# Moving hashes, turns and scalings between slots of a hand-written schedule (hash attention and a gated feed-forward, one core)

## The chip, the cores and the metric

The kernel runs on one core of one Trainium2 chip. Its five engines each work through a queue of their own, in order: TensorE (PE: matmuls and their weight loads), VectorE (DVE), ScalarE (ACT), GpSimd (POOL) and SyncE (SP), which here only issues DMAs. Semaphores order the queues among each other. The metric is the device time of one execution in microseconds, as the median of several runs.

## The reference

Inputs are q, k, v with 4 batches, 8 heads, 768 tokens and 64 values per head, a projection of 64 x 6, and the weights of a feed-forward block (512 to 1536 to 512).

```python
q_bits = (q @ proj > 0);  k_bits = (k @ proj > 0)      # 6 bits per token and head
mask   = bucket(q_bits)[..., :, None] == bucket(k_bits)[..., None, :]
scores = where(mask, q @ k.T / 8, -1e9)
attn   = softmax(scores)                               # 1e-9 added to the sum
x      = (attn @ v) as (4 * 768, 8 * 64)
xn     = x / sqrt(mean(x * x) + 1e-6) * rms_g
out    = (silu(xn @ w_gate) * (xn @ w_val)) @ w_out     # (3072, 512), float32
```

## The kernel before, in words

**Halves and slots.** Each batch b is done in two halves of 384 query tokens, w = 2b and 2b + 1, so there are eight halves. A *slot* is one of 192 steps: one head of one half, and one third p of the 768 keys (two blocks of 128). `SLOTS` lists them in order; heads go in pairs hp = 0 to 3. In the first four halves the pairs of two halves are interleaved (`TURNS`): half 2 takes slots 48 to 53 and 60 to 77, half 3 takes 54 to 59 and 78 to 95, and half 2 comes to pair 3 at slot 72. From half 4 on each half has 24 slots in a row. In step s the loop at the end of the kernel emits the scores of slot s + 1 (`scores`, two matmuls), then the planned work of rank below 3, then the exponentials of slot s + 1 (`probs`, ScalarE), then the rest of the plan by rank. Every engine's order follows from that list: `at(s, f, ...)` puts a piece of work into slot s. Nothing reorders it later.

**Masks by extra rows.** q and k stand transposed in a tile `QK` per pair: 64 rows of values and 12 rows of sign bits, scaled so that a score with a differing bit is pushed far down. The work on one pair (b, hp) before its first scores is:

- `load_blocks`: k and q as four DMAs each, issued by SyncE; v as one.
- `turn_dve`: eight transposes on VectorE, four for k and then four for q, one per slot (`in_row`), into `kT` and `qT`.
- `cast_pool`: copies to fp16 into `QK` on GpSimd; `v_prep` and `v_sum` there too.
- a hash: matmuls of `kT` and `qT` with the projection into a bank `d_ps` (line 210), their signs on VectorE (`bits`, line 217), then DMAs of the bits into the rows of `QK`, issued by SyncE. `hash_lone` (batch 1) hashes one pair with eight DMAs (line 285); `hash_pairs` (batches 2 and 3) hashes two pairs at once with eight (line 303).

`in_row(loads, s, hash_slot)` gives the slots: loads of k, q, v; turns at s to s + 7; casts at s + 4 and s + 8, v at s + 9; the hash at `hash_slot` (for batches 2 and 3 only at the odd pair, for both).

**Feed-forward.** When a half's eight heads are done, `attn_out` has divided by the softmax sum (`otmp`, `rcp` on VectorE, `x` and `sq` mostly on GpSimd); `norm` makes `rstd`; `scale_x` (VectorE, line 424) makes `xn`; `turn_x` transposes it on TensorE (`x_ps`) and VectorE writes `xnT`. From slot s0 = 24 w + 42 on, `gate` and `value` (lines 446 and 456) run over 12 blocks of columns between the scores of the following halves, from s0 + 16 on `project` (line 469), whose three results per half are copied by ScalarE to `ysb` and stored by a DMA that SyncE issues (line 478). So the first half's feed-forward starts at slot 42, its three stores are planned at slots 60, 63 and 66; the second half's starts at slot 66.

SyncE has all loads of q, k, v, all DMAs of bits and nearly all stores in one queue, in the order of the slots. GpSimd's queue issues the weight loads (lines 520 and 526).

Banks for `g_ps`, `v_ps`, `d_ps`, `x_ps`, `y_ps` and `m_ps` come from one pool of three; scores have two of their own, `o_ps` one.

Of the kernel before, what the change touches and what calls it, by code (L numbers as in the profile page):

```python
# [44 lines left out]
def kernel(  # L45
# [530 lines left out]
    def at(s, f, *a, rank=3):  # L576
        plan[s].append((rank, len(plan[s]), lambda: f(*a)))
# [55 lines left out]
    def in_row(loads, s, hash_slot=None):  # L633
        return loads, range(s, s + 8), (s + 4, s + 8, s + 9), hash_slot

    work = {
        (1, 1): in_row((21, 32, 33), 42, 50), (1, 2): in_row((38, 42, 44), 50, 58),
        (1, 3): in_row((46, 50, 53), 58, 66),
        (2, 0): in_row((56, 60, 62), 66), (2, 1): in_row((63, 67, 70), 74, 82),
        (2, 2): in_row((72, 75, 78), 82), (2, 3): in_row((80, 84, 87), 90, 98),  # L640
        (3, 0): in_row((90, 94, 98), 100), (3, 1): in_row((100, 104, 108), 110, 119),
        (3, 2): in_row((116, 120, 124), 126), (3, 3): in_row((126, 130, 134), 136, 145),
    }
# [34 lines left out]
    for w in range(8):  # L678
        for h in range(H):
            end = LAST[w, h] + 3  # L680
            at(end - 1, av, w, h, 0, 9)
            at(end, av, w, h, 9, 18)
            if h % 2:
                at(end, o_step, w, h // 2, rank=4.5)
                if (w, h) != (0, 7):
                    late = 3 if h == 7 and w < 3 else 5 if (w, h) == (0, 5) else 4
                    at(end + late, s_step, w, h // 2, rank=5 if late != 5 else 4)
        s0 = 24 * w + 42
        n0 = {0: 9, 2: 7}.get(w, 11)
        at(s0 - n0, norm, w, rank=5)  # L690
        for c in range(3):
            at(s0 - {0: 4, 2: 6 - c}.get(w, 8 - c), scale_x, w, c, rank=5)
            xs = {0: (2, 1, 1), 2: (4, 2, 1)}.get(w, (5, 3, 1))
            at(s0 - xs[c], turn_x, w, c, rank=1)
        seen = set()
        for ft in range(NF):
            for f, s in ((g_step, s0 + 16 * ft // NF), (v_step, s0 + (32 * ft + 16) // (2 * NF))):
                at(s, f, w, ft, rank=4 if s in seen else 2)
                seen.add(s)
        for i in range(9 if w < 7 else 6):  # L700
            c, j = divmod(i, 3)
            at(s0 + 16 + i, project, w, c, 4 * j, 4 * j + 4, rank=1 if i == 8 else 3)
# [61 lines left out]
```

## Time and profile before

| | |
|---|---|
| median of 3 runs | 346.21 us (344.65 to 346.27) |
| the profiled execution | 345.11 us, its span 343.3 us |
| TensorE busy | 330.0 us (96%) |
| VectorE, ScalarE, GpSimd busy | 238.6, 208.1, 156.4 us |
| granted TensorE clock, mean | 0.99 |

All times in the rows below are microseconds from the start of the span. A row of the timeline gives start, duration, engine, line, operation, what is written and read, and how many instructions are merged in it; in square brackets the idle time of the engine before it and what ended it. "SPq" is SyncE issuing DMAs: its duration is the issue, not the transfer. A row of the waits gives who waited for whom, the total, how often, and the longest. A row of the windows gives the stretch, then the busy time of PE, PEld, DVE, ACT and POOL, each with its number of instructions, then the granted clock, the DMA share and GB/s. In the chain of waits, a DMA piece runs from the start of its issue to its landing.

### The profile page before, as it was taken

Reading aid. Unit: us, or ns where it says so; the run is one execution under the profiler, and the core shown is the slowest. Engines: PE = TensorE matmul, PEld = TensorE weight load, DVE = VectorE, ACT = ScalarE, POOL = GpSimd, SP = SyncE. Lnnn points to the kernel's source line nnn. Section 1 sums busy time; section 2 is a strip of 40 time slices with the busy share of each in tenths; the row PEclk is TensorE's granted clock in tenths of the full one; section 3 lists DMA queues with packets and bytes.
Section 4 is the critical chain, followed back from the end, with each engine's and each line's share of the span. In section 5 each row is a group of like instructions: output and inputs, shape, how many; then the busy total and the mean of one; then the engine's idle time right before and its main releaser. Section 6 shows DMA issues by size and latency. Waiting matters only on the chain.

```text
span 343.3 us, 7798 instructions
## 1 busy us (share of the span) xinstructions
PE 330.0 (96%) x2983; PEld 201.4 (59%) x2983; DVE 238.6 (70%) x532; ACT 208.1 (61%) x324; POOL 156.4 (46%) x230
## 2 busy tenths in 40 slices
PE   8999979999969999999999999999999999999995
PEld 7566646555535645666565665656566656655653
DVE  4789669888564977788868695877446753784860
ACT  3789967665544745757666675667667765532322
POOL 4888775487631775636836156353101221130000
PEclk9999999999996999999999999999999999999999
DMA  7998939947375904803631373000010001001002
GB/s 239 324 235 183 139 57 186 161 78 141 72 170 112 170 7 96 193 5 85 148 83 29 63 140 107 33 6 13 32 61 2 3 31 63 0 3 61 32 0 92
DMA packets 85972, 31.36 MB, mean 91 GB/s; under 512 B 71480, under 2 KB 82992, under 8 KB 85936
## 3 DMA queue, kind: packets, MB, share of 16 engines
q1 hardware_dynamic: 82000, 26.09, 32.9%
q0 software_dynamic: 3712, 4.72, 9.1%
q8 instruction: 23, 0.38, 0.4%
q14 instruction: 13, 0.11, 0.1%
q10 hardware_dynamic: 224, 0.07, 0.1%
HBM read 28.32 MB, written 6.29 MB: 101 GB/s over the span
## 4 chain that ended last, share of the span: by engine, by line
PE 83%; DVE 8%; ACT 3%; SPq 2%; DMA 2%; issue 1%; DVEq 0%; ACTq 0%
PE v_ps L456 16%; PE y_ps L469 16%; PE s_ps L344 15%; PE g_ps L446 13%; PE o_ps L366 9%; PE d_ps L210 4%; PE s_ps L446 3%; ACT psb L354 2%; PE t_ps L170 2%; DVE t L457 1%; DVE ht L458 1%; DMA vL<-in_v_dram 1%; PE x_ps L431 1%; PE z_ps L337 1%; DVE kT L194 1%
## 5 line engine op out<-in xcount | busy, mean ns | idle before, releaser
L354 ACT ACTIVATE psb<-s_ps 128x768 f16<-128x768 f32 x192 | 150.6, 809 | 32.3 <-PE s_ps L344 30.3
L344 PE MATMUL s_ps<-QK 76*128 76x384 f16 x384 | 94.4, 328 | 4.9 <-DMA QK<-bits 3.0
L456 PE MATMUL v_ps<-xnT,wv 128*128 128x384 f16 x384 | 78.9, 328 | 0.0
L448 ACT ACTIVATE t<-g_ps 128x384 f32<-128x384 f32 x78 | 38.3, 491 | 54.0 <-PE g_ps L446 53.5
L469 PE MATMUL y_ps<-wo,ht 128*128 128x512 f16 x276 | 69.2, 379 | 0.0
L446 PE MATMUL g_ps<-xnT,wg 128*128 128x384 f16 x312 | 64.8, 330 | 1.3 <-DVE xnT L432 0.8
L366 PEld LDWEIGHTS <-psb 128*128 128x128 f16 x1152 | 52.4, 98 | 22.5 <-issue 4.7
L457 DVE SCALAR_TENSOR_TENSOR t<-t,g_ps 128x384 f32<-128x384 f32 x78 | 42.7, 548 | 32.3 <-ACT t L448 31.9
L390 POOL TENSOR_TENSOR x<-otmp,rcp 128x384 f32<-128x384 f32 x31 | 25.9, 837 | 82.1 <-DVE rcp L386 81.8
L458 DVE SCALAR_TENSOR_TENSOR ht<-t,v_ps 128x384 f16<-128x384 f32 x96 | 53.2, 554 | 11.9 <-PE v_ps L456 2.6
L366 PE MATMUL o_ps<-vl,psb 128*128 128x65 f16 x1152 | 57.0, 194 | 0.0
L446 PEld LDWEIGHTS <-wg 128*128 128x128 f16 x384 | 36.5, 98 | 26.0 <-issue 3.2
L456 PEld LDWEIGHTS <-wv 128*128 128x128 f16 x384 | 36.4, 98 | 24.7 <-issue 2.1
L344 PEld LDWEIGHTS <-QK 76*128 76x128 f16 x384 | 31.6, 98 | 21.8 <-issue 9.0
L469 PEld LDWEIGHTS <-ht 128*128 128x128 f16 x276 | 25.8, 97 | 24.8 <-issue 1.2
L202 POOL CAST QK<-qT 64x768 f16<-64x768 f32 x22 | 18.2, 829 | 26.6 <-DVE qT L194 23.8
L476 ACT COPY ysb<-y_ps 128x512 f32<-128x512 f32 x23 | 13.5, 587 | 24.4 <-PE y_ps L469 24.0
L402 POOL TENSOR_TENSOR sq<-x 128x384 f32<-128x384 f32 x31 | 25.8, 831 | 2.4
L432 DVE TENSOR_TENSOR xnT<-x_ps,gcol 128x512 f16<-128x512 f16 x24 | 16.2, 681 | 14.8 <-PE x_ps L431 14.8
L381 DVE TENSOR_TENSOR otmp<-o_ps,cvb 128x390 f32<-128x390 f32 x32 | 17.9, 559 | 9.9 <-PE o_ps L366 9.8
L202 POOL CAST QK<-kT 64x768 f16<-64x768 f32 x22 | 18.2, 826 | 10.6 <-PE v_ps L456 4.0
L194 DVE STREAM_TRANSPOSE kT<-kL 128x192 f32<-128x192 f32 x44 | 22.2, 519 | 0.0
(80 smaller groups left out, 304.6 us busy)
## 6 DMA issues: line engine op xcount, KB each, us to landing
vL<-in_v_dram SPq DMA_DIRECT2D x16, 384.0 KB
out_dram<-ysb SPq DMA_DIRECT2D x23, 256.0 KB
kL<-in_k_dram SPq DMA_DIRECT2D x44, 96.0 KB
qL<-in_q_dram SPq DMA_DIRECT2D x44, 96.0 KB
kL<-in_k_dram SPq DMA_DIRECT2D x4, 384.0 KB
qL<-in_q_dram SPq DMA_DIRECT2D x4, 384.0 KB
wg<-in_moe_w_gate_dram POOLq DMA_DIRECT2D x2, 768.0 KB, 7.4
wv<-in_moe_w_val_dram POOLq DMA_DIRECT2D x2, 768.0 KB, 8.1
```

The lines of the kernel that those rows point to most:

```text
L202: nc.gpsimd.tensor_copy(QK[b, hp][0:64, hh, o : o + S], T0[b, hp, which][64 * hh : 64 * hh + 64, :])
L344: nc.tensor.matmul(ps[:, j, 0:HALF], k_cols(w // 2, h, 2 * p + j), q_cols(w, h), start=True, stop=True,)
L354: nc.scalar.activation(psb[w, h][:, p], sps.pop(g)[:, :, 0:HALF], AF.Exp, scale=ESCALE,)
L366: nc.tensor.matmul(o[:, c, hh, 0:65], psb[w, h][:, jt // 2, jt % 2, 128 * c : 128 * c + 128], vls[b % 2][:, h, v_chunk(b, h, jt), 0:65], s ...
L390: eng.tensor_mul(xd.rearrange("p c (h d) -> p c h d", h=2), tmp[:, :, :, 0:64], r.to_broadcast([128, 3, 2, 64]),)
L402: nc.gpsimd.tensor_mul(sq, xd, xd)
L446: nc.tensor.matmul(g, wg[:, kt, fs], xnT[w][:, kt], start=(kt == 0), stop=(kt == 3))
L448: nc.scalar.activation(t, g, AF.Tanh, scale=0.5)
L456: nc.tensor.matmul(vv, wv[:, kt, fs], xnT[w][:, kt], start=(kt == 0), stop=(kt == 3))
L457: nc.vector.scalar_tensor_tensor(out=t, in0=t, scalar=1.0, in1=g, op0=ALU.add, op1=ALU.mult)
L458: nc.vector.scalar_tensor_tensor(out=ht[w][:, ft], in0=t, scalar=0.5, in1=vv, op0=ALU.mult, op1=ALU.mult)
L469: nc.tensor.matmul(y, ht[w][:, ft, c * 128 : (c + 1) * 128], wo[:, ft, :], start=(ft == 0), stop=(ft == NF - 1),)
```

## The change

Only slots in the plan change; the work itself is the same.

```diff
     work = {
-        (1, 1): in_row((21, 32, 33), 42, 50), (1, 2): in_row((38, 42, 44), 50, 58),
-        (1, 3): in_row((46, 50, 53), 58, 66),
-        (2, 0): in_row((56, 60, 62), 66), (2, 1): in_row((63, 67, 70), 74, 82),
-        (2, 2): in_row((72, 75, 78), 82), (2, 3): in_row((80, 84, 87), 90, 98),
+        (1, 1): in_row((21, 32, 33), 42, 51), (1, 2): in_row((38, 42, 44), 49, 58),
+        (1, 3): in_row((46, 52, 54), 56, 65),
+        (2, 0): in_row((56, 60, 62), 64), (2, 1): in_row((63, 66, 69), 72, 81),
+        (2, 2): in_row((71, 75, 78), 81), (2, 3): in_row((80, 83, 86), 89, 98),
         (3, 0): in_row((90, 94, 98), 100), (3, 1): in_row((100, 104, 108), 110, 119),
...
         for c in range(3):
-            at(s0 - {0: 4, 2: 6 - c}.get(w, 8 - c), scale_x, w, c, rank=5)
-            xs = {0: (2, 1, 1), 2: (4, 2, 1)}.get(w, (5, 3, 1))
+            at(s0 - {0: 5 - c // 2, 2: 6 - c}.get(w, 8 - c), scale_x, w, c, rank=5)
+            xs = {0: (3, 2, 1), 2: (4, 2, 1)}.get(w, (5, 3, 1))
             at(s0 - xs[c], turn_x, w, c, rank=1)
```

Each hash of batches 1 and 2 now stands two slots behind the last turn of its pair, where it stood one (except the double hash of (2,2) and (2,3), which moves from one to two as its turns move). For that the hash of (1,1) moves a slot later, those of (1,3) and of (2,0) with (2,1) a slot sooner, and the rows of turns of (1,2), (2,2) and (2,3) one slot, of (1,3), (2,0) and (2,1) two slots sooner; the casts and the preparation of v move with them. A few loads move by one or two slots. In SyncE's queue one thing changes places: the eight DMAs of the bits of (1,3) stand ahead of the first half's third store, which stood ahead of them.

For the first half (w = 0) two of the three scalings move from slot 38 to 37, ahead of the other half's `otmp` and `rcp` on VectorE; the third stays behind these at 38. The transposes move from slots 40, 41, 41 to 39, 40, 41.

## The prediction

> **What bounds the kernel now.** I read the page's head first, then TensorE's waits, then windows over the stretch where it waits longest, then the DMA queue of SyncE through that stretch.
>
> ```profile
> span 343.3 us, 7798 instructions
> PE 330.0 (96%) x2983; PEld 201.4 (59%) x2983; DVE 238.6 (70%) x532; ACT 208.1 (61%) x324; POOL 156.4 (46%) x230
> ...
> PE s_ps L344 <- DMA QK<-bits: 3.0, 1, 3.0
> PE s_ps L344 <- ACT psb L354: 1.4, 5, 0.4
> PE d_ps L210 <- DVE qT L194: 1.1, 2, 0.7
> ...
> PE g_ps L446 <- DVE xnT L432: 0.8, 1, 0.8
> PE x_ps L431 <- DVE xn L424: 0.6, 1, 0.6
> ...
> PE g_ps L446 <- DVE t L457: 0.4, 1, 0.4
> ...
> 99.00:102.30 3.30, 0.34 (x3) 0.11 (x2) 1.77 (x4) 0.56 (x1) 1.62 (x2) 0.94 0.40 141
> 102.30:109.30 7.00, 7.00 (x33) 3.54 (x33) 2.44 (x5) 3.07 (x5) 0.00 (x0) 0.54 0.37 61
> ...
> 150.00:200.00 50.00, 50.00 (x471) 30.46 (x469) 37.95 (x82) 32.61 (x51) 26.02 (x36) 1.00 0.38 82
> ```
>
> TensorE is busy 96% of the span, so a step counts only where it takes away an idle stretch of TensorE or a slow one. The waits (columns: total us, times, longest) are few, and four of the six quoted stand where the change moves work: `x_ps` and `g_ps` at slots 40 to 42, `d_ps` at the two hashes whose last turn is one slot ahead of them, and `s_ps` waiting 3.0 us for sign rows of a hash. The windows (TensorE's busy time is the second number, the granted clock the third from the end) show that this last wait costs twice: behind it the clock is 0.54 for 7.00 us, in which TensorE is busy throughout. At full clock that work takes 0.54 x 7.00 = 3.78 us, so the slow stretch costs 3.22 us beside the wait's 2.96. From 150 us on TensorE is simply full: time won before stays won.
>
> Why that one wait ends when it does is the question on which the forecast turns:
>
> ```profile
> 98.45 0.81 PE L456 MATMUL v_ps<-xnT,wv 128*128 128x384 f16 x4
> 102.22 0.80 PE L344 MATMUL s_ps<-QK 76*128 76x384 f16 x2 [2.96 <-DMA QK<-bits]
> ...
> 76.95 2.71 SPq L122 DMA_DIRECT2D qL<-in_q_dram  x4
> 79.76 0.59 SPq L112 DMA_DIRECT2D vL<-in_v_dram  x1
> 80.45 3.10 SPq L122 DMA_DIRECT2D kL<-in_k_dram  x4
> 83.67 6.21 SPq L285 DMA_DIRECT2D QK<-bits  x8
> 89.92 2.71 SPq L122 DMA_DIRECT2D qL<-in_q_dram  x4
> 92.72 0.58 SPq L478 DMA_DIRECT2D out_dram<-ysb  x1
> 93.35 0.42 SPq L112 DMA_DIRECT2D vL<-in_v_dram  x1
> 93.87 3.38 SPq L122 DMA_DIRECT2D kL<-in_k_dram  x4
> 97.36 1.06 SPq L478 DMA_DIRECT2D out_dram<-ysb  x2
> 98.50 6.61 SPq L285 DMA_DIRECT2D QK<-bits  x8
> ...
> 98.04 0.38 SPq L478 DMA_DIRECT2D out_dram<-ysb  x1
> ...
> 91.92 0.68 DVE bits L217
> ...
> 100.20 1.88 DMA QK<-bits
> ```
>
> The bits of pair (1,3) are there at 91.92 + 0.68 = 92.60. Their eight DMAs start to be issued at 98.50. In between SyncE is not waiting, it is issuing: each row begins where the one before ends, back to 76.95 and beyond. The scores need the third of the eight, whose issue starts at 100.20 and which has landed 1.88 us later, at 102.08. So the wait is ended by a queue 5.9 us behind its data, not by the hash.
>
> **The change, part by part.**
>
> *Scalings of the first half (scale_x(0, 0) and (0, 1) from slot 38 to 37, turn_x a slot sooner).*
>
> ```profile
> 43.95 0.89 POOL L419 TENSOR_TENSOR rstd<-ms,mhalf 128x3 f32<-128x3 f32 x1
> 45.32 0.56 DVE L381 TENSOR_TENSOR otmp<-o_ps,cvb 128x390 f32<-128x390 f32 x1 [1.83 <-PE o_ps L366]
> 46.03 2.38 DVE L424 TENSOR_SCALAR xn<-x,rstd 128x512 f16<-128x512 f32 x3
> 48.34 1.87 DVE L432 TENSOR_TENSOR xnT<-x_ps,gcol 128x512 f16<-128x512 f16 x3
> ...
> 50.26 0.81 PE L446 MATMUL g_ps<-xnT,wg 128*128 128x384 f16 x4 [0.80 <-DVE xnT L432]
> ...
> L424 DVE TENSOR_SCALAR xn<-x,rstd x24: 402/484/1057, 46.0 to 310.1; 128x512 f16<-128x512 f32 x24
> ```
>
> VectorE stands idle 1.83 us ahead of the other half's `otmp`, and rstd is ready at 44.84. Put first, two scalings run there at 0.40 to 0.48 us each (the shortest and the median of the 24), to about 45.8; `otmp` and the reciprocal follow to 46.55, 0.45 later than now, the third scaling to about 47.1, the three `xnT` (1.87) to about 49.1. The first gate starts near 49.15 instead of 50.26: 1.1 us won, between 0 (if `otmp`, 0.45 late, holds back the next half) and 1.4 (both idle times of the page's rows above, 0.6 and 0.8). It reaches the end only if nothing behind it waits for something else, and the wait at 102.22 does.
>
> *Hash of pair (1,1) at slot 51 instead of 50, that of (1,2) still at 58 with its turns a slot sooner.* The second takes the smaller of the two `d_ps` waits away, 1.1 - 0.7 = 0.4 us, ahead of 102.22 as well. The first costs nothing: its bits are there at 64.09 + 0.68 = 64.77 and SyncE issues them from 69.87, so a slot more (well under 2 us) is hidden there.
>
> ```profile
> 64.09 0.68 DVE L217 TENSOR_SCALAR bits<-d_ps,thr,scl 128x384 f16<-128x384 f32 x1 [0.96 <-PE d_ps L210]
> ...
> 69.87 6.98 SPq L285 DMA_DIRECT2D QK<-bits  x8
> ```
>
> In slots 42 to 57 VectorE gets 18 turns for 16; two more at some 0.5 us each fit into what TensorE has won there.
>
> *Hash of pair (1,3) at slot 65, turns from 56.* The bits come about 3 us sooner, which SyncE does not notice. What it notices is the order: the third store of the first half (slot 66) now stands behind the eight DMAs instead of ahead of them. They start 98.50 - 98.04 = 0.46 sooner, and so does the landing: the wait ends near 101.76. The lower bound is 0 (one of the two weight loads on the other queue, issued sooner, takes transfer time from SyncE's loads), the upper 1.06, both stores' issue. I take 0.46, by the row itself. The other loads keep their order on SyncE; (1,3)'s q and v loads go from 50 and 53 to slots 52 and 54, the q load now behind (1,1)'s hash as it was.
>
> TensorE meets the wait with 1.1 + 0.4 us more in hand. So the idle stretch begins near 97.7 instead of 99.26 and is about 4.0 us long; what was won before 98 goes into it, with no gain at the end.
>
> *The q turns of (1,3), slots 60 to 63 instead of 62 to 65,* come close to their load. Its last issue ends at 79.66; the nearest landing is the 1.88 from issue start to data, so it is there at 80.9 (the v load's 4.35 in the chain would make it 83.4). The turn of slot 60, now the third k turn of (1,3), stands at 80.41, after the change near 78.9. VectorE can wait 2.0 us there, at most 4.5, with the third scaling and an `otmp` behind it. TensorE has the 4.0 us stretch in front of it: cost 0, as long as less than that is passed on.
>
> ```profile
> 135.36 4.35 DMA vL<-in_v_dram
> ...
> 80.41 0.52 DVE L194 STREAM_TRANSPOSE kT<-kL 128x192 f32<-128x192 f32 x1
> ...
> 121.72 0.53 DVE L457 SCALAR_TENSOR_TENSOR t<-t,g_ps 128x384 f32<-128x384 f32 x1
> ...
> 123.39 0.51 PE L210 MATMUL d_ps<-qT,pq 128*32 128x384 f32 x1 [0.69 <-DVE qT L194]
> ...
> SPq L303 <- DVE kT L194: 8.2, 1, 8.2
> ```
>
> *Batch 2: turns of (2,0) to (2,3) one or two slots sooner, the double hash at slot 81 instead of 82.* Here the wait of 0.69 at 123.39 goes: the last q turn is two slots ahead. Late next is the second bank, free when `t` has been formed (121.72 + 0.53 = 122.25), while TensorE would have finished the first bank at about the same time. So I take 0.6, bounds 0 and 0.69. It is behind the SyncE wait, and TensorE is full from there on, so it stays. SyncE itself idles 8.2 us at that hash now: its DMAs a slot sooner cost nothing. The hash of (2,2) and (2,3) stays at 98 and had no wait. On GpSimd the preparation of v of (2,3) goes ahead of one normalisation; that engine has idle time on both sides, cost 0.
>
> *The clock.* The slow stretch was worth 3.22 us. I leave it as it is, with 1.6 either way (half of it): the idle time ahead of it grows, its end does not move by more than 0.46.
>
> The Trainium skill (TensorE: Matmul & The Clock Gate, Part 1) says that the gate halves the clock after an idle window of about 3.4 us, counted freely, and lifts it after a busy one. The trace agrees on the halving (0.50 to 0.54), though here 2.96 us of idle time were already enough. By that rule a stretch longer than a window is throttled in every run, where a shorter one may slip between two windows.
>
> **Sum.** 345.11 (span 343.30 and 1.81 around it) - 0.46 - 0.6 = 344.05, with 1.1 + 0.4 won and lost again in the SyncE wait. The median of the runs shown is 346.21, 0.3% above the profiled one; 0.997 of it is 345.1. I forecast 345.1. Its own range: lower 343.0 (1.06 + 0.69 and the clock 1.4 better), upper 347.0 (nothing won, clock 0.8 worse).
>
> **Rivals.**
> - *The wait goes altogether.* If the hash, not the queue, were late, 2.96 + 3.22 + 0.6 would go: 338.3, or 339.4 by the median. For it: the hash is done 3 us sooner. Against it: the eight DMAs would have to start some 4 us sooner, and SyncE's rows leave 0.46. A tenth.
> - *The longer idle stretch holds the clock down longer (slower).* Place: from 97.7. The low clock lasted some 7 us; if it lasts another such stretch, TensorE loses 0.46 x 7.00 = 3.2 more: 347.3, by the median 348.4. It decides once the extra slow time is over 2 x 1.06 us. For it: 4.0 us is a third more than what brought the throttle on. Against it: the added idle time is itself spent before the matmuls resume, so part of the slow time falls into it. 0.13.
> - *VectorE's wait for (1,3)'s q load is passed on.* It decides beyond 4.0 us of delay; at the 4.5 bound, with the two extra turns, 1.5 us are left: about 346.6 by the median's scale if the gains stay, 347.7 if the 0.6 and 0.46 go too. Against: TensorE there runs projections and scores, which do not read VectorE's turns. 0.09.
> - *The main case,* a small gain from an order of two DMAs and one hash: 0.68.
>
> **The numbers.** Half a per cent, 1.73 us, is about what a measurement can tell. Faster by more (below 344.5): the first rival 0.10 and three tenths of the main case, 0.20. Slower by more (above 347.9): the clock 0.10, VectorE 0.04, main 0.02. The rest, 0.54, is within. For the range I leave out the first rival's 0.10 and some 0.09 at the top: 341.5 to 348.0.
>
> **What would show it.** Right: SyncE's eight DMAs for (1,3) start near 98.0 with one store ahead of them; `s_ps` waits about 4 us for them; the first gate starts near 49.2; no `d_ps` wait on qT. Wrong: an `s_ps` wait shorter than 2.9 us, which would mean that SyncE's queue follows the work it serves; a low clock of over 8 us; a `g_ps` or `o_ps` wait on VectorE between 80 and 97 that outlasts the DMAs.

## The result and the profile after

| | before | after |
|---|---|---|
| median of 20 runs each | 344.31 us (340.43 to 346.27) | 340.82 us (339.42 to 343.79) |
| profiled execution | 345.11 us, span 343.3 | 340.95 us, span 339.2 |
| granted clock, mean | 0.990 | 0.995 |

After takes 0.9917 of before, 95% interval 0.9892 to 0.9943: 0.8% faster. The forecast was 345.1 (341.5 to 348.0), so the time lies below the range.

The head of after's page, and TensorE's waits:

```profile
span 339.2 us, 7797 instructions
PE 326.1 (96%) x2983; PEld 200.2 (59%) x2983; DVE 237.7 (70%) x532; ACT 207.9 (61%) x324; POOL 155.6 (46%) x230
...
PE d_ps L210 <- DVE t L457: 3.5, 1, 3.5
PE s_ps L344 <- DMA QK<-bits: 1.3, 2, 1.1
...
PE g_ps L446 <- DVE xnT L432: 0.6, 1, 0.6
```

Windows of after (columns as in the prediction) over its new wait on `d_ps`, the stretch ahead of slot 72, the 7 us behind it, and all from the scores of slot 72 to the end:

```profile
66.70:71.00 4.30, 4.27 (x27) 1.98 (x28) 3.84 (x9) 0.81 (x1) 2.74 (x4) 0.60 0.95 190
99.00:102.30 3.30, 1.81 (x18) 1.06 (x18) 2.97 (x8) 1.19 (x2) 1.38 (x2) 1.00 0.30 96
102.30:109.30 7.00, 6.77 (x63) 4.34 (x63) 4.52 (x11) 4.28 (x7) 4.33 (x6) 1.00 0.33 75
102.23:339.20 236.97, 232.91 (x2032) 140.76 (x2032) 162.03 (x338) 139.28 (x222) 87.23 (x116) 1.00 0.28 62
```

The last of these windows in before:

```profile
102.22:343.30 241.08, 236.71 (x2032) 142.29 (x2032) 161.89 (x338) 139.53 (x222) 87.39 (x116) 0.99 0.26 59
```

The scores of slot 72 begin at 102.22 before and 102.23 after. Everything won ahead of them is gone by then. All of the profiled gain lies behind: 241.08 - 236.97 = 4.11 us, with the same 2032 matmuls.

The timelines of after, of TensorE, SyncE and VectorE:

```profile
48.54 0.81 PE L446 MATMUL g_ps<-xnT,wg 128*128 128x384 f16 x4 [0.57 <-DVE xnT L432]
66.73 0.56 PE L210 MATMUL d_ps<-kT,pk 128*32 128x384 f32 x1 [3.48 <-DVE t L457]
102.23 0.49 PE L344 MATMUL s_ps<-QK 76*128 76x384 f16 x2 [1.07 <-DMA QK<-bits]
118.76 0.51 PE L210 MATMUL d_ps<-kT,pk 128*32 128x384 f32 x1
120.53 1.03 PE L469 MATMUL y_ps<-wo,ht 128*128 128x512 f16 x4
...
50.45 8.08 SPq L122 DMA_DIRECT2D kL<-in_k_dram  x4
79.33 4.38 SPq L122 DMA_DIRECT2D kL<-in_k_dram  x4
94.09 3.69 SPq L122 DMA_DIRECT2D kL<-in_k_dram  x4
97.88 0.58 SPq L478 DMA_DIRECT2D out_dram<-ysb  x1
...
65.77 0.52 DVE L194 STREAM_TRANSPOSE kT<-kL 128x192 f32<-128x192 f32 x1 [4.33 <-issue]
```

The chain of after at the new wait:

```profile
55.60 5.84 DMA kL<-in_k_dram
61.44 4.33 issue
65.77 0.52 DVE kT L194
```

The same turn in the timeline of before:

```profile
66.57 0.89 DVE L194 STREAM_TRANSPOSE kT<-kL 128x192 f32<-128x192 f32 x2
```

GpSimd's issue of the second of the two loads of `w_out` (768 KB each), in the timelines of before and of after:

```profile
59.41 0.89 POOL L526 DMA_DIRECT2D wo<-in_moe_w_out_dram  x1
```

```profile
57.72 0.89 POOL L526 DMA_DIRECT2D wo<-in_moe_w_out_dram  x1
```

Here is the wait that the prediction didn't have. The first k turn of (1,2) stands one slot sooner (49), and TensorE reaches that slot 1.7 us sooner. The turn needs all four k loads of its pair, which are issued from 50.45 to 58.53. The chain goes back to the last of them, though it names nothing for the last 4.33 us. The semaphore records in the trace do: the fourth load's last step comes at 65.69, and VectorE's queue is held ahead of this turn until 65.72. So VectorE stands idle for those 4.33 us, a `t` and the hash of (1,1) are queued behind the turn, and TensorE waits 3.48 us at 66.73 and then runs at a clock of 0.60. Before, the turn started at 66.57, later than it does now, and without idle time.

The slot alone doesn't make this wait. By the same records the fourth load had landed at 61.64 in before; a turn ready at 61.44, as it is in after, would have waited 0.2 us for that. In after it lands 4.05 us later. What stands otherwise around it is the weight load of the two rows above: it too comes 1.69 us sooner, and so before the fourth k load's issue has ended (58.53; in before the issue had ended at 58.38, ahead of the weight load). In the nine profiled kernels with the scalings moved, the weight load is issued at 57.59 to 58.10, and the k load lands at 65.67 to 66.76 in eight of them, at 61.61 in the ninth (e10 below). In the six without, it is issued from 58.79 on, and the k load has landed by 61.74 in all. That the weight load holds the k load up is argued from this order; no run moves it alone.

The stall costs nothing at the end, since the scores of slot 72 start at 102.2 anyway. It only takes up the time that was won, and more: at slot 72 there are 1.07 us left to wait instead of 2.96, and the clock behind is 1.00.

The starts of the 96 gates in order, after less before, show the same as a running account: -1.7 us at gates 1 to 7, +3.2 at 9 to 12 (the new wait), -0.26 at the gate at 102.81, -2.76 from the gate at 109.86 to the 24th, -4.00 at the 25th, -4.15 from the 32nd to the end. So 2.76 us come from the clock behind slot 72 (the scores there start at the same time), 1.23 from the stretch with the hash at slot 81, and about 0.14 from one near the hash at slot 98. The loss of the clock at 66.7 isn't in the sum, as it falls ahead of the wait.

### The profile page after: what moved, and what is told of

It reads as the page before. It is cut to its first block, busy times and chain, and to the rows that moved or that the text cites. A ratio compares the mean times of both kernels' runs of the same rounds, so it can differ in the third digit from the quotient of the medians.

```text
span 339.2 us, 7797 instructions
## 1 busy us (share of the span) xinstructions
PE 326.1 (96%) x2983; PEld 200.2 (59%) x2983; DVE 237.7 (70%) x532; ACT 207.9 (61%) x324; POOL 155.6 (46%) x230
## 3 DMA queue, kind: packets, MB, share of 16 engines
HBM read 28.32 MB, written 6.29 MB: 102 GB/s over the span
## 4 chain that ended last, share of the span: by engine, by line
PE 80%; DVE 8%; POOL 3%; DMA 3%; SPq 2%; issue 2%; ACT 1%; DVEq 0%; ACTq 0%; POOLq 0%
PE y_ps L469 18%; PE v_ps L456 16%; PE s_ps L344 14%; PE g_ps L446 13%; PE o_ps L366 8%; PE d_ps L210 4%; PE s_ps L446 3%; DMA kL<-in_k_dram 2%; PE x_ps L431 1%; SPq L122 1%; SPq L285 1%; PE z_ps L337 1%; PE t_ps L170 1%; DMA QK<-bits 1%; DVE t L457 1%
## 5 line engine op out<-in xcount | busy, mean ns | idle before, releaser
L446 PE MATMUL g_ps<-xnT,wg 128*128 128x384 f16 x312 | 63.5, 325 | 1.2 <-DVE xnT L432 0.6
```

The costliest lines, as they stand in the source:

```text
L446: nc.tensor.matmul(g, wg[:, kt, fs], xnT[w][:, kt], start=(kt == 0), stop=(kt == 3))
```

## The experiments

Three theories. *Queue:* the scores of slot 72 are released by SyncE's queue; what is won ahead of them is lost, and gains come only from the clock behind and from later steps. *Parts:* each part keeps its own gain to the end. *Stall:* the new wait at 66.73 costs time, and without it the change would be worth far more.

### Which part brings it

**e1_scalings: before, with the scalings' part alone.**

```diff
-            at(s0 - {0: 4, 2: 6 - c}.get(w, 8 - c), scale_x, w, c, rank=5)
-            xs = {0: (2, 1, 1), 2: (4, 2, 1)}.get(w, (5, 3, 1))
+            at(s0 - {0: 5 - c // 2, 2: 6 - c}.get(w, 8 - c), scale_x, w, c, rank=5)
+            xs = {0: (3, 2, 1), 2: (4, 2, 1)}.get(w, (5, 3, 1))
```

> The kernel before with the scalings of the first half alone moved. Queue theory (the scores of slot 72 start at about 102.2 us whatever is won ahead of them, since SyncE's queue brings their sign rows; what counts is whether a long idle stretch ends there and leaves a low clock behind it): the first gate starts near 48.6 instead of 50.26, the scores of slot 72 still between 101.5 and 102.8, with an idle stretch of 2.5 us or more and the low clock behind it; time against before 0.995 to 1.005. Stall theory (each wait taken away gains its own length): 1.7 us faster, 0.995, with the scores of slot 72 near 100.5.

343.47 us, 0.9978 [0.9950, 1.0006]. The first gate starts at 48.62, 1.64 us sooner. The timeline of this kernel at slot 72, and the window behind:

```profile
101.84 0.80 PE L344 MATMUL s_ps<-QK 76*128 76x384 f16 x2 [3.48 <-DMA QK<-bits]
```

```profile
101.84:108.84 7.00, 7.00 (x41) 3.88 (x42) 2.44 (x6) 3.13 (x5) 0.00 (x0) 0.59 0.33 55
```

The wait is longer than the 2.96 of before, the scores start only 0.38 sooner, and the clock behind is low as before. Of the 1.64 us won, 0.52 went into this wait, as the queue theory has it. Another 0.74 was lost ahead of it, most of it at the turns of (1,2): they still stand at slot 50 here, but their k load lands late (65.91), and VectorE waits 1.03 us for it.

**e2_batch1: before, with the rows of (1,1), (1,2), (1,3) alone.**

```diff
-        (1, 1): in_row((21, 32, 33), 42, 50), (1, 2): in_row((38, 42, 44), 50, 58),
-        (1, 3): in_row((46, 50, 53), 58, 66),
+        (1, 1): in_row((21, 32, 33), 42, 51), (1, 2): in_row((38, 42, 44), 49, 58),
+        (1, 3): in_row((46, 52, 54), 56, 65),
```

> The kernel before with the rows of turns and hashes of batch 1 alone moved. Queue theory: VectorE's first turn of pair (1,2), a slot sooner, waits for its k load, TensorE waits for VectorE near 65 us, and the idle stretch at the scores of slot 72 is under 2 us with no low clock behind it; these scores start at 101.5 to 102.8; some 3 us faster, 0.989 to 0.994. Stall theory: the d_ps wait of 0.4 us goes, 0.999.

343.45 us, 0.9976 [0.9947, 1.0006]: less than expected. Without the scalings the k load of (1,2) is there in time (61.56): its first turn, at slot 49 as in after, starts at 62.60 without a wait. So the move of the turns alone doesn't stall VectorE, and the wait at slot 72 stays at 2.56 us. In the profiled execution the clock didn't drop behind it, as the timelines of VectorE and TensorE and the window show:

```profile
62.60 0.54 DVE L194 STREAM_TRANSPOSE kT<-kL 128x192 f32<-128x192 f32 x1
...
101.65 0.48 PE L344 MATMUL s_ps<-QK 76*128 76x384 f16 x2 [2.56 <-DMA QK<-bits]
```

```profile
101.65:108.65 7.00, 7.00 (x65) 4.50 (x66) 4.25 (x9) 4.28 (x7) 1.59 (x2) 1.00 0.39 85
```

That execution has a span of 339.7, but most runs of this kernel have a lower mean clock, so the median gains little.

**e3_batch2: before, with the rows of batch 2 alone.**

```diff
-        (2, 0): in_row((56, 60, 62), 66), (2, 1): in_row((63, 67, 70), 74, 82),
-        (2, 2): in_row((72, 75, 78), 82), (2, 3): in_row((80, 84, 87), 90, 98),
+        (2, 0): in_row((56, 60, 62), 64), (2, 1): in_row((63, 66, 69), 72, 81),
+        (2, 2): in_row((71, 75, 78), 81), (2, 3): in_row((80, 83, 86), 89, 98),
```

> The kernel before with the rows of batch 2 alone moved (double hash at slot 81). Both theories: the d_ps wait of 0.69 us near 123 goes, nothing else moves; 0.998, with the idle stretch and the low clock at the scores of slot 72 as in the kernel before. If batch 2 carries the gain, 0.992.

342.70 us, 0.9951 [0.9921, 0.9982], more than expected. Between the 24th and the 25th gate it gains 1.23 us, as the whole change does. The scores of slot 72 even start later than before here (103.12, after 3.80 us). The three parts add up to -0.22 - 0.24 - 0.49 = -0.95%, the whole is -0.83%. Each interval is about 0.3% either way, so the parts add up within the noise; batch 2's is the only one of the three that is clear of 1. These times alone don't tell the theory of parts from that of the queue; e1's rows do.

**e8_hash82: before, with the turns of (2,1) one slot sooner and the hash left at slot 82**.

```diff
-        (2, 1): in_row((63, 67, 70), 74, 82),
+        (2, 1): in_row((63, 67, 70), 73, 82),
```

> The kernel before with one row alone changed: pair (2,1) turns from slot 73 instead of 74, its hash still at 82, so two slots behind the last turn. The wait of 0.69 us near 123 goes, and with it 0.5 us in which the four matmuls of that hash did not run side by side: 1.2 us between the twelfth gate of the second half and the first gate of the third (17.77 in the kernel before, 16.5 here). The scores of slot 72 as before. If the place of the hash between value and projection matters, not the wait, then 17.8.

344.63 us in its one run, span 342.9. From the 24th to the 25th gate it gains 0.72, not the 1.2 expected: the `d_ps` wait is gone, but an `x_ps` wait of 0.57 has come at 129.96. The first of the bank's sixteen matmuls (four run side by side) and the projection behind them, in the timeline of this kernel and then of before:

```profile
122.11 0.51 PE L210 MATMUL d_ps<-kT,pk 128*32 128x384 f32 x1
...
123.60 1.04 PE L469 MATMUL y_ps<-wo,ht 128*128 128x512 f16 x4
```

```profile
121.85 0.51 PE L210 MATMUL d_ps<-kT,pk 128*32 128x384 f32 x1
...
124.80 1.04 PE L469 MATMUL y_ps<-wo,ht 128*128 128x512 f16 x4
```

The stretch takes 123.60 - 122.11 = 1.49 us here and 124.80 - 121.85 = 2.95 before, where only 0.69 was shown as a wait. In after it takes 120.53 - 118.76 = 1.77. In before six of the sixteen ran ahead of the wait and ten behind it. So the wait and the split together cost nearer 1.2 to 1.5 us than 0.69; how the rest comes about, the rows don't say.

### Is it the clock?

**e4_filler and e4b_filler: before, with 40 idle matmuls (the kernel's own filler, line 337) ahead of the scores of slot 72.** Their results are used by nothing.

```diff
-{0: 8, 3: 6}.get(g, 0)
+{0: 8, 3: 6, 72: 40}.get(g, 0)
```

> The kernel before with 40 idle matmuls of 128 columns put ahead of the scores of slot 72 (the helper that the kernel has for its start), nothing else moved. Queue theory: the scores of slot 72 start at about 102.2 as before, TensorE is busy until shortly before, the clock stays at 1.0 behind it, and the 3.2 us of slow work go: 0.989 to 0.993, as much as the whole change. Stall theory: no wait is shorter, so 1.000, or slower by what the fillers take.

> The kernel before with the 40 idle matmuls ahead of the scores of slot 72, once more for a profile. The scores still start between 101.6 and 103.1; the idle time of TensorE ahead of them is under 1 us; no low clock behind them; the gates after them follow at the pace of the full clock. Time 0.994 to 0.999 against before, as the first look at this edit had it.

343.32 us, 0.9968 [0.9937, 0.9998], and 343.61 us, 0.9966 [0.9926, 1.0006]. The trace of the first has a clock of 0.66 from end to end, so no row of it is read. The second, its timeline and the window behind:

```profile
98.31 2.40 PE L337 MATMUL s_ps<-ones 128*128 128x128 f16 x40
103.41 0.80 PE L344 MATMUL s_ps<-QK 76*128 76x384 f16 x2 [2.70 <-DMA QK<-bits]
104.00 1.49 PE L446 MATMUL g_ps<-xnT,wg 128*128 128x384 f16 x4
```

```profile
104.00:108.00 4.00, 4.00 (x21) 2.17 (x20) 0.61 (x2) 1.95 (x3) 0.00 (x0) 0.50 0.26 43
```

The expectation of less than 1 us of idle time was missed: the fillers ran early, the DMAs came later in this execution, and 2.70 us were left, with the low clock behind them. Over all the runs it is clearer. The mean clock of a run comes in steps of about 0.005, which is 0.005 x 340 = 1.7 us. In the traces that is one stretch of 3.41 us at half the clock; before has two of them behind slot 72 (101.93 to 108.76), after one behind its new wait. Counted in such steps:

| mean clock | before: runs, median | after: runs, median |
|---|---|---|
| 0.998 and over | 12, 341.78 us | 2, 339.74 us |
| about 0.995 | 46, 344.04 us | 11, 340.95 us |
| about 0.990 | 32, 345.56 us | 7, 340.91 us |

These are the 92 runs of before that stand beside the experiments; two more of them have 0.985, at 347.3 and 348.4 us. In before a step costs 1.5 to 2.3 us. In after there are as many steps (1.25 per run), but in the medians the second costs nothing; that fits the profile, where one falls ahead of the wait at slot 72. The fillers cut the steps from 1.26 per run to 0.36 and 0.7 and brought 0.3%, at the edge of the noise and less than the steps' price: at full clock they themselves cost something (their runs without a step have medians of 342.75 and 342.43 us, against 341.78). That the clock makes up part of the gain is shown by the table and the profiles together; the fillers alone don't show how much.

### Does the new stall cost anything?

**e5_turn50: after, with the turns of (1,2) back at slot 50, the hash at 59.**

```diff
-        (1, 2): in_row((38, 42, 44), 49, 58),
+        (1, 2): in_row((38, 42, 44), 50, 59),
```

> The changed kernel with one row put back: pair (1,2) turns from slot 50 again (hash at 59), so that VectorE no longer waits for its k load and TensorE no longer for VectorE near 63 us (3.48 us in the changed kernel). Queue theory: what is won there is lost at the scores of slot 72, which start at 101.5 to 103.1 as in all kernels so far, with 3 us or more of idle time ahead and a low clock behind, where it counts: 1 to 2 us slower than the changed kernel, 0.993 to 0.998 against before. Stall theory: 3.5 us and its low clock gained, 0.978 to 0.983.

341.59 us, 0.9910 [0.9880, 0.9940]: as fast as after. But the edit didn't take the stall away. The load of (1,2), landed at 66.76, still holds VectorE up, for 2.80 us, and the bits of (1,1) behind it hold TensorE for 2.25. So the 0.978 to 0.983 of the stall theory weren't put to the test. What the run shows is that TensorE's wait near 67 is 1.23 us shorter than in after, and that at slot 72 is 1.89 us longer:

```profile
66.84 0.52 DVE L194 STREAM_TRANSPOSE kT<-kL 128x192 f32<-128x192 f32 x1 [2.80 <-DMA kL<-in_k_dram]
67.87 0.81 PE L446 MATMUL g_ps<-xnT,wg 128*128 128x384 f16 x4 [2.25 <-DVE bits L217]
102.69 0.49 PE L344 MATMUL s_ps<-QK 76*128 76x384 f16 x2 [2.96 <-DMA QK<-bits]
```

### Can the queue be relieved?

**e6_act and e7_act_turn50: after, and after with e5's edit, with the k and q loads of (2,0) issued by ScalarE.**

```diff
+            if which != "v" and (b, hp) == (2, 0):
+                at(s, load_blocks, nc.scalar, b, hp, which)
+                continue
```

> The changed kernel with the eight k and q loads of pair (2,0) issued by ScalarE (same slots, 56 and 60) instead of SyncE. Queue theory: SyncE reaches the sign rows of (1,3) 5 to 6 us sooner, near 93; the scores of slot 72 then start when TensorE gets there, 101.2 instead of 102.23, and later stages keep the 1 us: 0.986 to 0.990 against before. Should the queue not be what holds them, nothing moves: 0.992.

> Both edits: (2,0)'s k and q loads on ScalarE's queue and (1,2)'s turns at slot 50, hash at 59. Queue theory: with the queue no longer behind, the 3.48 us at 63 and the low clock after them now count, so the edit that loses alone wins here: scores of slot 72 start at 97 to 99, no slow window there; 0.974 to 0.984 against before. If the two edits only added (1 us gained and 1.5 lost), 0.990 to 0.995.

344.22 us, 1.0015 [0.9988, 1.0042], and 344.95 us, 1.0035 [1.0011, 1.0060]: 1% slower than after. SyncE was relieved, but the issue now stands in ScalarE's queue, whose activations TensorE needs. Of e7, ScalarE's queue and activations, then TensorE:

```profile
75.47 4.25 ACTq L122 DMA_DIRECT2D kL<-in_k_dram  x4
79.83 0.49 ACT L448 ACTIVATE t<-g_ps 128x384 f32<-128x384 f32 x1 [6.29 <-DMA kL<-in_k_dram]
...
81.23 0.80 PE L344 MATMUL s_ps<-QK 76*128 76x384 f16 x2 [5.00 <-issue]
```

For the queue theory these two settle nothing, as they put a new bound in place of the old one.

**e9_noload: e5 with the q load of (2,0) left out.** The q turns of (2,0) read its k tile instead, so that part of the scores is another one.

```diff
-        src = raw[b, hp, which]
+        src = raw[b, hp, "k" if (b, hp) == (2, 0) else which]
...
+            if (b, hp, which) == (2, 0, "q"):
+                continue
```

> The kernel with (1,2)'s turns at slot 50 (its scores of slot 72 at 102.69 behind 2.96 us of idle time), and the four q DMAs of pair (2,0) left out: that pair's q is turned from its k tile, so its scores are not the reference's, with the same work on every engine but SyncE. Queue theory: the eight sign DMAs of (1,3) start 2.7 us sooner, near 96.3, the scores of slot 72 at 99.7 to 100.3, idle under 0.8 us, no low clock behind: 0.980 to 0.986 against before. If something else held these scores, they stay at 102 to 103 and the time at 0.991.

336.47 us, 0.9770 [0.9732, 0.9808], better than expected. The DMAs of (1,3)'s bits start at 94.10, TensorE waits for bits 0.19 us at most, and no run has a low clock. Four loads fewer on SyncE bring 1.4% against e5, where the whole change brought 0.8%. In the profile VectorE's wait for (1,2)'s k load is still there (landed at 65.67), with 1.35 us of it left on TensorE.

**e10_late: e5 with the first half's first two stores and the v load of (2,0) moved behind those DMAs, to slot 66.** Nothing is left out. TensorE waits for none of the three; once the v load is moved, GpSimd waits 3.58 us for it, up to 105.19.

```diff
+    def late_stores():
+        for dst, src in held_out:
+            nc.sync.dma_start(out=dst, in_=src)
...
-            nc.sync.dma_start(out=rows[:, out_chunk(w, c), :], in_=ysb)
+            if w == 0 and c < 2:
+                held_out.append((rows[:, out_chunk(w, c), :], ysb))
+            else:
+                nc.sync.dma_start(out=rows[:, out_chunk(w, c), :], in_=ysb)
...
-        (2, 0): in_row((56, 60, 62), 64),
+        (2, 0): in_row((56, 60, 66), 64),
...
+    at(66, late_stores)
```

> The kernel with (1,2)'s turns at slot 50, and three DMAs that nobody waits for moved behind the sign DMAs of (1,3) on SyncE's queue: the first half's first two stores and the v load of (2,0). Nothing is left out. Queue theory: those sign DMAs start 1.8 us sooner, near 97.2, the scores of slot 72 at 100.6 to 101.3, idle 1 to 1.6 us, a low clock behind it rarely: 0.983 to 0.989, better than both kernels. If the wait were for anything but the queue, 0.991.

**336.44 us, 0.9780 [0.9738, 0.9822]**: faster than both kernels. Its span, TensorE's wait for bits, and SyncE's queue:

```profile
span 334.8 us, 7797 instructions
...
PE s_ps L344 <- DMA QK<-bits: 0.2, 1, 0.2
```

```profile
88.75 2.71 SPq L122 DMA_DIRECT2D qL<-in_q_dram  x4
91.50 2.72 SPq L122 DMA_DIRECT2D kL<-in_k_dram  x4
94.33 6.17 SPq L285 DMA_DIRECT2D QK<-bits  x8
100.60 0.61 SPq L485 DMA_DIRECT2D out_dram<-ysb  x1
...
104.83 1.23 SPq L466 DMA_DIRECT2D out_dram<-ysb  x2
```

The two stores of L466 are the ones moved; L485 is the first half's third. In this execution (1,2)'s k load landed at 61.61, and VectorE didn't wait for it.

**e11_wide: e10, with (1,2)'s bits in four DMAs of 768 columns instead of eight** (its hash over two banks).

```diff
-                at(sh, hash_lone, b, hp)
+                at(sh, hash_wide if hp == 2 else hash_lone, b, hp)
```

> The same, and the hash of (1,2) over two banks so that its sign rows need four DMAs of 768 columns instead of eight of 384: 2.9 us less on SyncE's queue, 0.8 us more on TensorE and 0.6 us more on VectorE at slot 59. Queue theory: sign DMAs of (1,3) start near 94.3, the scores of slot 72 when TensorE gets there, 100.3 to 100.9, no idle time over 0.5 us: 0.982 to 0.988, no better than moving the three DMAs alone by more than 0.003, since what the queue gives back TensorE has paid at the hash.

336.69 us, 0.9774 [0.9734, 0.9814]. The DMAs of (1,3) start at 92.88, 1.45 sooner again, and it brings nothing. TensorE no longer waits there, so a shorter queue has nothing left to give; that the hash over two banks costs TensorE what the queue gives back, as expected, would look the same.

**e12_before_late and e13_after_late: e10's edit of the three DMAs on before and on after.**

> The kernel before with the first two stores and the v load of (2,0) moved behind the sign DMAs of (1,3), without any of the change's moves. Queue theory: those DMAs start 1.7 us sooner or more, the scores of slot 72 at 99.3 to 100.7 with under 1.4 us of idle time and hardly a low clock behind: 0.984 to 0.991 against before. The waits at 48 to 50, 76 and 123 us stay, so it is slower than the kernel that has both by 2 to 4 us. If the change's moves carried the 0.978 of that kernel, and not the queue, this one stays within 0.995 to 1.000.

> The changed kernel, (1,2)'s turns at slot 49 and its hash at 58 as it has them, with the same three DMAs moved behind. Queue theory: the 3.5 us that TensorE waits near 63 and the low clock after them are no longer taken up by a later wait, so they count: scores of slot 72 at 100.5 to 101.5, 2 to 4 us slower than with the turns at slot 50, 0.984 to 0.990 against before; the same difference of one slot was worth nothing (0.991 and 0.992) while the queue was behind. Stall theory: the one-slot difference is worth the same here as there, nothing: 0.978.

339.73 us, 0.9877 [0.9828, 0.9925], and 337.77 us, 0.9832 [0.9779, 0.9886]. The timelines of e12, then timeline and window of e13. The e13 execution shown is the slowest of its six (340.45 us); four of the six have a mean clock of 0.998 or more, at 336.74 to 337.83 us, so what it shows of the clock isn't the usual case:

```profile
96.84 6.19 SPq L285 DMA_DIRECT2D QK<-bits  x8
100.50 0.48 PE L344 MATMUL s_ps<-QK 76*128 76x384 f16 x2 [1.02 <-DMA QK<-bits]
```

```profile
66.79 0.85 PE L210 MATMUL d_ps<-kT,pk 128*32 128x384 f32 x1 [3.65 <-DVE t L457]
```

```profile
66.79:71.00 4.21, 4.21 (x25) 1.79 (x26) 3.62 (x9) 0.81 (x1) 2.68 (x4) 0.50 1.00 200
```

| ratio to before | old order of SyncE | three DMAs moved |
|---|---|---|
| before's slots | 1 | 0.9877 |
| the change | 0.9917 | 0.9832 |
| the change, turns of (1,2) at 50 | 0.9910 | 0.9780 |

The table and e12's rows settle the queue theory. Three DMAs that TensorE doesn't wait for, moved on the kernel before, let the scores of slot 72 start 1.72 us sooner and bring 1.2% without any of the change. What the new stall is worth is less sure. With the three DMAs moved, turns at slot 49 are 337.77 - 336.44 = 1.3 us slower in the medians than turns at 50, but the intervals overlap. And with the old order after and e5 both have a stall, of 3.48 and 2.25 us on TensorE, so their equal times don't compare a stall with none. That it is free under the old order rests on the profiles: the scores of slot 72 start at 102.22 in before without it and at 102.23 in after with it.

## Why the prediction was wrong, point by point

- **The wait at slot 72 is ended by SyncE's queue, and the gains ahead of it are lost in it:** right. Both kernels start those scores at 102.2, e1 loses 0.52 of its 1.64 us there, and e12 shows the queue as the cause. The rival in which the wait goes altogether did not come about.
- **The scalings:** right in kind, mis-sized: first gate at 48.54 instead of 49.15, as the first two scalings fit almost wholly into VectorE's idle stretch (`otmp` starts 0.22 later, not 0.45). None of it reached the end.
- **The order of two DMAs, 0.46 us:** wrong, it was 0. One store fewer stands ahead of the DMAs, as said, but the two k loads ahead took longer to issue (4.38 for 3.10, 3.69 for 3.38), and they start at 98.56 against 98.50. The lower bound was 0, for another reason: a weight load on the other queue. The last weight load is issued at 57.72, some 20 us ahead of these k loads.
- **"Two more [turns] at some 0.5 us each fit into what TensorE has won there":** this is the step that failed. It counted VectorE's work and didn't ask when the k load of (1,2) lands; that was asked only for the q load of (1,3), where VectorE then waited for nothing. The turn was ready at 61.44, its load landed at 65.69, and VectorE stood still for 4.33 us. The load's row of before wouldn't have warned of that, as it landed at 61.64 there; what the prediction had named elsewhere, a weight load that is issued sooner and delays SyncE's loads, is the likely reason here. So the idle time did not grow to 4.0 us at slot 72; most of it came at 66.7.
- **The clock, left at 3.22 us "as it is":** wrong as a result of that, and the largest term that the sum lacks: 2.76 us. With 1.07 us of idle time at slot 72 the clock stays up behind it, and the low clock at 66.7 is paid out of time that would have been waited anyway. The prediction named a wait under 2.9 us as what would refute it, but gave it another cause, a queue that follows its work.
- **"A stretch longer than a window is throttled in every run":** this doesn't follow from windows that are counted freely and have to be idle as a whole, as a stretch of 4.0 us can lie across the edge of two. The traces have it so all the same: TensorE waits 3.42 us or more seven times in the profiled kernels, and the clock is low behind each. The last section shows why: an idle half of a window is about enough.
- **The hash at slot 81, 0.6 with an upper bound of 0.69:** mis-sized, 1.23. The bound took the wait's row for the cost of the wait, and the row leaves out what the split of the side-by-side matmuls costs.
- **The slower rival, a longer low clock:** didn't come about. With less idle time at slot 72 instead of more, it had no occasion.
- **The base, "346.21, 0.3% above the profiled one":** the median of three runs. Over 20 runs the kernel before has 344.31. Of the 345.1 - 340.8 = 4.3 us by which the forecast missed, 1.9 are this base and some 2.4 the change itself: 0.997 was forecast and 0.9917 measured. On the base of 344.31 the range would have held the time. The table by mean clock shows why three runs say little here: a run moves by 1.5 to 2.3 us with each step.

In the profiled executions the change was worth 4.16 us where 0.46 + 0.6 = 1.06 was forecast: nothing for the order of the two DMAs, 2.76 for the clock behind slot 72, 1.23 for the hash at 81, and some 0.14 near the hash at 98. What stays open: at the same mean clock after is 2.0 us (at full clock, two runs of after) to 3.1 us (one step) faster, and the hashes at 81 and 98 explain 1.37 of it. If the one step of after falls ahead of slot 72, as in its profile, 1.7 us of clock are free, and 1.37 + 1.7 = 3.1 is what was measured; but only one run of after is profiled. In the profiled kernels that have the old order of SyncE, slot 72 started anywhere between 101.65 and 103.41, and the runs don't tell how much of the rest that is.

## What to carry to other kernels

A wait that a queue ends is a wall: what is won ahead of it is lost, and what is lost ahead of it is free, a low clock included; so ask of each gain and each loss on which side of the wall it lies. Before moving work ahead of such a wall, read what stands in the queue that ends it, and move DMAs that nobody waits for behind the ones that release it: three of them brought 1.2% here, at least as much as seven moved rows. And a step moved sooner has to be set against the landing of its load, each of them: in a queue without gaps the loads don't come sooner with it, and one came 4.05 us later here, when a load of another queue did come sooner.

## What the runs showed of the hardware

- **What lowers the clock is the idle time within one step of a fixed grid, not the length of the gap.** Behind waits of 1.02 and 1.07 us it stayed at 1.00 (e12, after); behind 2.56 it stayed in e2; behind 2.70 it was 0.50 (e4b), behind 2.96 it was 0.54 (before), behind 3.65 it was 0.50 (e13). In the traces of the profiled kernels the low clock lasts 3.41 us or twice that within the kernel, and the drops of one trace lie whole multiples of 3.41 us apart. On that grid, two steps of e6 and then two of e5, as windows:

```profile
87.54:90.95 3.41, 1.57 (x18) 0.87 (x16) 1.45 (x4) 1.68 (x3) 1.12 (x2) 1.00 0.77 139
90.95:94.36 3.41, 3.41 (x13) 1.58 (x12) 1.46 (x3) 2.03 (x4) 2.06 (x3) 0.50 1.02 243
```

```profile
66.37:69.79 3.42, 1.92 (x20) 1.26 (x20) 2.85 (x7) 1.08 (x2) 2.18 (x4) 1.00 0.76 173
69.79:73.20 3.41, 3.41 (x34) 2.16 (x31) 3.20 (x8) 1.94 (x5) 1.64 (x2) 1.00 0.77 130
```

In e6 a wait of 1.84 us lies within one step and the next step runs at half the clock. In e5 a wait of 2.25 us is cut by a step's edge at 66.37, leaves 1.50 us idle in this step, and lowers nothing. From 20 us on, in the fourteen of these traces in which the clock drops, each of the 16 steps at full clock with 1.84 us or more idle is followed by a low clock, and none of those with 1.72 or less. The 2.56 us of e2 were split into 1.49 and 1.44: that they cost nothing was luck. The Trainium skill (TensorE: Matmul & The Clock Gate, Why this matters for your kernels) asks for no idle gap above about 3 us; here that leaves out gaps of 1.84, 2.70 and 2.96 us that did lower it.
- **Waits on one of several matmuls side by side cost more than their row.** 0.69 us shown, 1.2 to 1.5 us lost.
- **Issuing a load isn't free for the engine that issues it.** Four loads of 96 KB took ScalarE 4.25 us in e7, and its next activation came after 6.29 us without one. The Trainium skill (DMA: Bandwidth & Descriptors, Issuing engines are not separate DMA queues) says that spreading DMAs over engines only saves issue time; here it moved that time onto an engine that TensorE needs, at a cost of 1%.
